# Attention and a residual MLP on one core: a stage's last scalings, nine places for W2's chunks, lam's rows, and the second pass's relus

## The chip, the core and the metric

The kernel runs on one core of a Trainium2 chip. The core has five engines with a queue each: TensorE (PE in the profile, its weight loads PEld), VectorE (DVE), ScalarE (ACT), GpSimd (POOL) and SyncE (SP). POOL and SP issue nearly all DMAs. The metric is the device time of one execution in microseconds, the median of several runs. All durations below are microseconds unless they say ns.

## What is computed

For each of 8 batches, grouped-query attention (16 query heads, 4 key/value heads, 384 positions, head size 64), then an MLP block with residuals on the 384 x 1024 result:

```python
scores = q @ k.T / sqrt(64); attn = softmax(scores); x = attn @ v     # per batch and head
a1 = alpha1 * x + beta1
tok = einsum('ts,bsd->btd', w_tok, a1)
u = x + lam * tok
a2 = alpha2 * u + beta2
ch = maximum(a2 @ w_ch1, 0) @ w_ch2        # 1024 -> 4096 -> 1024
out = u + lam * ch
```

`lam`, `alpha1`, `beta1`, `alpha2` are vectors of 1024. Inputs and the output are float32; the kernel multiplies in bfloat16 and accumulates in float32.

## The kernel before

Five stages run one after the other: `main(0)` and `main(1)` compute the wide MLP of batches 0 and 1, then `pair(0)`, `pair(1)`, `pair(2)` compute that of batches (2,3), (4,5), (6,7). Each stage is a generator that yields after every few matmuls, 0 in its first half (the product with W1) and 1 in its second (the product with W2). A plan written out by hand (`put`, `put_all`) says at which yield the attention work of a later batch is recorded. The instruction order of every engine is the order of recording; nothing is moved by a scheduler.

**The first two stages.** `main(b)` takes W1 in 16 chunks of two 128-column tiles. For each tile, 8 matmuls of 128 x 384 (L531) fill one of two PSUM banks, and a relu with bias writes `hT`: on ScalarE (L540) when the tile's number is even and no exps are near (the counter `exps` is set to 2 by each exp of the attention and counted down by each tile), else on VectorE (L542). TensorE can start a tile only when the relu of the tile before last has freed its bank. In `main(0)` the table `turns` also places small jobs: `to_all` spreads half a row of lam, beta1 or alpha2 over all partitions (a VectorE stream shuffle, L927, of a row that SP loaded at L923), `load_row_set` loads the next such row, `k_transpose` and `q_transpose` turn keys and queries of batch 1 on TensorE. The places count yields: the first four tiles have one yield each (0 to 3), every later tile has two.

**The pair stages.** A pair's two batches are multiplied together, with seven products of half-size blocks instead of eight. The first half runs over eight groups `g`; a group has 14 tiles in the order of `SEQ1`, each of 4 matmuls of 128 x 384 (L724), with products numbered 1 to 7. `LEFT1` names the sum of the left side that a product reads: product 3, the tenth tile, reads `opb(6)`, which VectorE makes at L741, recorded at the fourth tile of group 0. The right sides of group `g+1` are made from two W1 chunks by `sum_w1` (L621, L626) at the tiles 3, 6, 9 and 12 of group `g`. VectorE and ScalarE add up the products (L729 to L737) and make the hidden blocks (L708, L709, L750 to L754). Product 7's and product 4's bank `Y` of the next group is free when L737 is done.

The second half multiplies the hidden blocks with W2 in the order 1, 2, 6, 5, 3, 7, 4 (`PLACE2`), 28 chunks of 512 KB, three row blocks `ms` each (L786). W2's blocks and their sums were written to DRAM tiles `w2s` earlier and are fetched again in each pair stage (L637, on SP). VectorE adds each result (L818 to L825); four of the products give a finished block of the output each. Such a block is scaled by lam in place (L688, 128 x 512 float32) and added to the output in DRAM by an accumulating DMA (`store`, L516, on POOL). Both are put into the list `later` and made one at a time at later points of the second half (`flush(1)`), and all that are left at the stage's end (`flush()`, L831).

**The places.** `w1` has 6 ring places of 512 KB, shared by W1's chunks (loaded on POOL at L185) and W2's. Two more, in `pad`, take every chunk whose number leaves 6 or 7 when divided by 8. `pad`'s 6 parts of 1024 columns also hold the sums of `sum_w1`. `queue` lists all loads in order and `pump` issues its head whenever a place of the right kind is free; while the head has none, the rest waits. Two W1 chunks of the next stage (`heads`) stand before the last two W2 chunks; the next two follow at the head of the next stage's list. Place by place they get their room as the product before is finished.

**What the attention puts in between.** In the pair stages' second half, scores (L279), exps (L288), the product with v (L315), the token product (L340) and their VectorE steps (L320 to L351) are placed between groups of four matmuls, and SP issues DMA transposes and writes of `u` beside the fetches.

Of the kernel before, what the change touches and what calls it, by code (L numbers as in the profile page):

```python
# [12 lines left out]
def kernel(  # L13
# [45 lines left out]
    RING = 6  # L59
# [33 lines left out]
    pad = const.tile([P, 2 * NST * DM], bf, tag="pad", name="pad")  # L93
# [17 lines left out]
    SLOTS = 7 * NH // 4  # L111
# [117 lines left out]
    def side(b):  # L229
# [201 lines left out]
        if not first:  # L431


            turns = {}
            if b == 1:
                turns = {4: [(to_all, 3, 0, 0), (to_all, 3, 1, 1), (load_row_set, 1, 1, 0), (load_row_set, 2, 0, 1)],
                         8: [(k_transpose, 0)], 12: [(to_all, 1, 0, 2), (to_all, 1, 1, 0), (load_row_set, 2, 1, 0)],
                         16: [(scale_beta,)], 20: [(to_all, 2, 0, 1), (to_all, 2, 1, 0)],
                         24: [(q_transpose, 0, 2, "av")], 28: [(k_transpose, 2)]}
                for i in range(3):  # L440
                    turns[32 + 4 * i] = [(q_transpose, 2 + 2 * i, 2, "av")]
            if (b - NPL) // 2 > 0:
                at = {}

                def put(k, *m):
                    at.setdefault(k, []).append(m)

                for j in range(6):
                    put((0, 6, 12, 21, 26, 31)[j], scores3, j, j in (2, 5))
                for p in range(NP):  # L450
                    put((4, 10, 14, 18, 24, 29, 33, 35)[p], av, p)
                    put((8, 15, 17, 22, 27, 32, 36, 38 if b % 2 else 39)[p], tok_flip, p)
                    if by_pe(p):
                        put((36, 39, 41)[p - NP + 3], turn, p)
                return turns, at
            return turns, {
                0: [(scores3, 0)], 4: [(av, 0)], 6: [(scores3, 1)], 8: [(tok_flip, 0)], 11: [(av, 1)],
                13: [(scores3, 2, True)], 15: [(av, 2)], 16: [(tok_flip, 1)], 18: [(tok_flip, 2)], 19: [(av, 3)],
                21: [(scores3, 3)], 23: [(tok_flip, 3)], 25: [(av, 4)], 27: [(scores3, 4)], 29: [(tok_flip, 4)],
                31: [(av, 5)], 33: [(scores3, 5, True)], 35: [(av, 6), (tok_flip, 5)], 37: [(av, 7)],  # L460
                38: [(tok_flip, 6)], 41: [(tok_flip, 7)],
                **{39 + 4 * i - i // 2 * 2: [(turn, p)] for i, p in enumerate((5, 6, 7)) if by_pe(p)}}
# [57 lines left out]
    def main(b):  # L520
# [4 lines left out]
        for i, c in enumerate(seq):  # L525
            for j in range(CW):
                nt = c * CW + j
                begun = b == 0 and nt in early
                ps = early[nt] if begun else bank([P, 512], "mm", "h")
                for dt in range(0 if begun else NDT):  # L530
                    nc.tensor.matmul(out=ps[:, :n], lhsT=w1[:, w1_slots[c], dt, j * P:(j + 1) * P],  # L531
                                     rhs=a2T[:, dt, :n], start=(dt == 0), stop=(dt == NDT - 1))
                    if dt == 3:
                        yield 0
                c1 = bias1[:, nt:nt + 1]
                if b == 0:
                    evac("DVE" if nt % 2 else "ACT")(out=c1, in_=ps[:, S:n])
                exps[0] -= 1
                if nt % 2 == 0 and exps[0] < 0:
                    nc.scalar.activation(out=hT[:, nt, :], in_=ps[:, :S], func=RELU, bias=c1)  # L540
                else:
                    nc.vector.tensor_scalar(out=hT[:, nt, :], in0=ps[:, :S], scalar1=c1,  # L542
                                            scalar2=0.0, op0=ADD, op1=mybir.AluOpType.max)
                yield 0
            if i + RING < NCH:
                w1_free.append(w1_slots.pop(c))
                load_w1(seq[i + RING])

            if b == 0 and i == NCH - RING:
                for dw, r, h in [(0, 1, 1)] + [(0, r, h) for r in (2, 3) for h in range(2)] + [  # L550
                        (1, r, h) for r in range(4) for h in range(2)]:
                    load_w2(dw, r, h)
                load_next(2)
# [74 lines left out]
    NB = (B - NPL) // 2  # L628
    w2_slots, w2_at = {}, {}

    def padded(n):
        return n % 8 > 5

    def fetch(i, n):
        w2_slots[i, n] = slot = (pad_free if padded(n) else w1_free).pop(0)
        w2_at[i, n] = ring[:, slot] if slot < RING else pad[:, (slot - RING + 1) * 2048:(slot - RING + 2) * 2048]
        nc.sync.dma_start(out=w2_at[i, n], in_=w2s[n])  # L637

    def free(slot):
# [3 lines left out]
    def pump():  # L643
        while queue:
            f, *a = queue[0]
            if not (pad_free if f == fetch and padded(a[1]) else w1_free):
                return
            queue.pop(0)
            f(*a)

    pad_free = []
    queue = []
    for i in range(NB):
        heads = [(load_w1, c) for c in order1[:2]] if i + 1 < NB else []
        queue += [(load_w1, c) for c in order1[2 if i else RING:]] + [(fetch, i, n) for n in range(SLOTS - 2)] + heads
        queue += [(fetch, i, n) for n in (SLOTS - 2, SLOTS - 1)]

    IDENT = mybir.ActivationFunctionType.Identity
    SEQ1 = ((1, 0), (1, 1), (7, 0), (6, 0), (6, 1), (7, 1), (5, 0), (5, 1), (2, 0), (3, 0), (3, 1), (2, 1), (4, 0), (4, 1))
    LEFT1 = {1: 3, 2: 4, 3: 6, 4: 1, 5: 2, 6: 5, 7: 0}  # L660
    LEFT2 = {1: 0, 2: 4, 3: 4, 4: 1, 5: 3, 6: 0, 7: 2}

    pair_banks = ExitStack()

    def share_banks(*names):
        pair_banks.close()
# [4 lines left out]
    def pair(i):  # L671
# [19 lines left out]
        def flush(n=9):  # L691
            while later and n:
                f, *a = later.pop(0)
                f(*a)
                n -= 1

        later = []
        last = i == NB - 1

        def sums_hid(o, r):  # L700
# [10 lines left out]
        for g in range(NH // 2):  # L711
            X, Y, snap = {}, {}, {}
            for k, (o, e) in enumerate(SEQ1):
# [16 lines left out]
                if o == 5:  # L730
                    tt(out=hid[:, t, 1], in0=Y[e][:, :S], in1=snap[5, e], op=ADD)
                elif o == 2:
                    tt(out=hid[:, t, 0], in0=ps, in1=snap[1, e], op=ADD)
                elif o == 3:
                    nc.scalar.activation(out=hid[:, t, 4], in_=ps, func=RELU, bias=hi)
                elif o == 4:
                    tt(out=hid[:, t, 2], in0=ps, in1=snap[6, e], op=ADD)  # L737
                if (o, e) in ((2, 1), (3, 1)):
                    free(w1_slots.pop(g if o == 2 else g + NCH // 2))
                if k == 3 and g == 0:  # L740
# [26 lines left out]
        for k, o in enumerate(PLACE2):  # L767
            whole = not last and o != 4
            for h in range(1 if whole else 2):
                for ms in range(NST):  # L770
# [13 lines left out]
                    for (c0, c1, x), t in ((c, t) for c in X[ms] for t in range(8 * h, upto)):  # L784
# [12 lines left out]
                        if t % 4 == 3 and t < upto - 1 and c1 == 512:  # L797
                            q = 4 * ms + t // 4
                            if whole and o in (2, 6) and q in (2, 5, 8, 10):
                                sums_hid(o, (2, 5, 8, 10).index(q))  # L800
                            if t % 8 == 3:
                                flush(1)
                            yield 1
                    if k == ms == h == 0:
                        pad_free[:] = [RING, RING + 1]
                        pump()
                    if (whole or h == 1) and not (last and o == 4):
                        if o in (1, 6, 5):
# [19 lines left out]
                    if last and o in (2, 6) and (h, ms) in ((0, 1), (0, 2), (1, 0), (1, 1)):  # L828
                        sums_hid(o, [(0, 1), (0, 2), (1, 0), (1, 1)].index((h, ms)))
                    yield 1  # L830
        flush()  # L831

    order = {mybir.EngineType.PE, mybir.EngineType.DVE, mybir.EngineType.Activation,
             mybir.EngineType.Pool, mybir.EngineType.SP}
# [221 lines left out]
```

## Time and profile before

| what | value |
|---|---|
| runs | 742.67, 743.75, 743.16; median 743.16 |
| profiled execution | 742.75, its span 741.0 |
| busy, share of the span | PE 98%, DVE 70%, PEld 56%, ACT 43%, POOL 22% |
| `main(0)`, `main(1)` | to about 132, to about 243 |
| `pair(0)`, `pair(1)`, `pair(2)` | from about 243, 416 and 591 |
| DMA | 151.32 MB, mean 204 GB/s |
| busy from 205 to 230, then 230 to 338 | DVE 18.13 of 25; 86.26 of 108 |

A matmul's end is modelled, so TensorE's busy share does not say that it runs at its peak. Lines of the timeline give the start, the time to the end of the last of a run, the engine, the line of the kernel, the operation, what it writes and reads, the count, and in brackets the idle time before it with what ended it. Lines of the waits give the total, the number of times and the longest. POOL's and SP's queues hold DMAs that wait for what they read and for the place they write; a DMA that waits holds up those behind it in its queue.

### The profile page before, as it was taken

How to read it: one execution, taken by the hardware profiler on the slowest of the kernel's cores; microseconds unless marked ns; L12 is line 12 of the kernel's file. 1: busy time of each engine (PE TensorE's matmuls, PEld its weight loads, DVE VectorE, ACT ScalarE, POOL GpSimd, SP SyncE). 2: the span in 40 equal slices, each digit the busy share in tenths (PEclk: the TensorE clock that was granted, in tenths of full speed). 3: DMA queues.
4: the chain of work that ended last, by engine and by line, in shares of the span. 5: the costliest groups of instructions: out<-in, count | busy, mean ns of one | idle time of the engine just before them, and what ended most of it. 6: DMA issues, size and time to landing. Idle time of an engine off the chain costs nothing.

```text
span 741.0 us, 14454 instructions
## 1 busy us (share of the span) xinstructions
PE 727.3 (98%) x5710; PEld 418.0 (56%) x5769; DVE 521.7 (70%) x1004; ACT 319.5 (43%) x458; POOL 163.4 (22%) x211
## 2 busy tenths in 40 slices
PE   8999999999999999999999999999999999999997
PEld 5856555666555566655555556655555556654444
DVE  7863366577687889749777977747958987762354
ACT  7622431434332566653334366664343256660000
POOL 9434220420000232211011533210002231000011
PEclk9999999999999999999999999999999999999999
DMA  9999999999998999999979999998999999936975
GB/s 187 194 201 200 207 218 175 186 198 181 221 271 244 182 221 213 252 248 211 281 186 251 152 196 180 196 205 199 266 238 201 195 179 119 158 120 231 289 219 97
DMA packets 218018, 151.32 MB, mean 204 GB/s; under 512 B 88661, under 2 KB 197061, under 8 KB 217949
## 3 DMA queue, kind: packets, MB, share of 16 engines
q0 software_dynamic: 120304, 64.60, 66.3%
q1 hardware_dynamic: 97100, 85.39, 41.7%
q8 instruction: 45, 0.74, 0.4%
q10 hardware_dynamic: 544, 0.39, 0.2%
q14 instruction: 25, 0.20, 0.1%
HBM read 154.84 MB, written 38.27 MB: 261 GB/s over the span
## 4 chain that ended last, share of the span: by engine, by line
PE 81%; DMA 7%; DVE 5%; issue 4%; POOL 3%; POOLq 0%; DVEq 0%
PE C L786 24%; PE X L724 15%; PE ch L569 10%; PE h L531 10%; PE Y L724 8%; PE sc L279 4%; PE Z L724 4%; PE sc L315 3%; DMA w<-in_moe_w_ch_dram 3%; PE sc L340 3%; DMA q_raw<-in_q_dram 2%; DMA ops<-a 1%; POOL w L185 1%; DVE xr L323 1%; DMA rows<-in_moe_lam_dram 1%
## 5 line engine op out<-in xcount | busy, mean ns | idle before, releaser
L288 ACT ACTIVATE es<-sc 128x1024 bf16<-128x1024 f32 x126 | 121.4, 1023 | 161.8 <-PE sc L279 150.5
L786 PE MATMUL C<-w,arena 128*128 128x512 bf16 (+2 forms) x779 | 179.6, 373 | 1.8 <-issue 0.3
L786 PEld LDWEIGHTS <-arena 128*128 128x128 bf16 x1040 | 94.7, 98 | 100.5 <-issue 5.1
L729 ACT ACTIVATE hT<-X,bias 128x384 f32<-128x384 f32 x144 | 83.9, 582 | 62.2 <-PE X L724 55.0
L724 PEld LDWEIGHTS <-w 128*128 128x128 bf16 x768 | 75.0, 98 | 51.8 <-DVE ops L741 1.6
L569 PE MATMUL ch<-arena,hT 128*128 128x512 bf16 x366 | 87.9, 379 | 1.0 <-issue 0.3
L185 POOL DMA_DIRECT2D w<-in_moe_w_ch_dram x68 | 61.4, 910 | 123.2 <-PE X L724 70.9
L516 POOL DMA_DIRECT2D out_dram<-hT x33 | 29.1, 883 | 265.3 <-DVE hT L688 91.9
L531 PE MATMUL h<-ops,w 128*128 128x384 bf16 (+1 forms) x480 | 83.3, 327 | 1.6 <-DVE hT L542 1.5
L724 PEld LDWEIGHTS <-pad 128*128 128x128 bf16 x576 | 56.3, 98 | 37.8 <-issue 0.8
L724 PE MATMUL X<-ops,w 128*128 128x384 bf16 x384 | 70.3, 326 | 0.8 <-DVE ops L741 0.8
L724 PE MATMUL X<-ops,pad 128*128 128x384 bf16 x384 | 70.3, 326 | 0.0
L531 PEld LDWEIGHTS <-w 128*128 128x128 bf16 x480 | 45.4, 98 | 31.2 <-issue 2.4
L569 PEld LDWEIGHTS <-hT 128*128 128x128 bf16 x384 | 34.8, 98 | 36.8 <-issue 2.5
L786 PE MATMUL C<-pad,arena 128*128 128x512 bf16 (+2 forms) x220 | 52.5, 371 | 0.2
L347 DVE TENSOR_TENSOR xr<-sc,xr 128x384 f32<-128x384 f32 x56 | 30.9, 553 | 22.8 <-PE sc L340 22.8
L315 PEld LDWEIGHTS <-es 128*128 128x128 bf16 x1008 | 38.3, 97 | 12.4
L340 PEld LDWEIGHTS <-wtokT 128*128 128x128 bf16 x576 | 37.5, 98 | 11.8 <-DVE a L330 0.8
L279 PE MATMUL sc<-qT,kT 64*128 64x384 bf16 (+2 forms) x576 | 41.8, 271 | 1.8 <-ACT hT L288 0.2
L320 DVE RECIPROCAL rinv<-sc 128x6 f32<-128x6 f32 x56 | 10.8, 192 | 42.5 <-PE sc L315 42.3
L315 PE MATMUL sc<-v,es 128*128 128x65 bf16 x1008 | 39.8, 193 | 0.0
L724 PE MATMUL Y<-ops,w 128*128 128x384 bf16 x192 | 39.4, 326 | 0.3 <-DVE arena L737 0.3
(138 smaller groups left out, 909.1 us busy)
## 6 DMA issues: line engine op xcount, KB each, us to landing
w<-in_moe_w_ch_dram POOLq DMA_DIRECT2D x68, 512.0 KB, 10.4
w<-w2s SPq DMA_DIRECT2D x66, 512.0 KB, 4.9
out_dram<-xr SPq DMA_DIRECT2D x56, 192.0 KB, 5.9
pad<-w2s SPq DMA_DIRECT2D x18, 512.0 KB, 7.6
out_dram<-hT POOLq DMA_DIRECT2D x33, 256.0 KB, 5.8
arena<-in_moe_w_ch_dram POOLq DMA_DIRECT2D x16, 512.0 KB, 19.8
w2s<-arena SPq DMA_DIRECT2D x28, 256.0 KB, 3.6
q_raw<-in_q_dram POOLq DMA_DIRECT2D x28, 192.0 KB, 11.0
```

What stands on the lines that cost most here:

```text
L185: nc.gpsimd.dma_start(out=w1[:, w1_slots[c]], in_=w1src[:, :, c * CW * P:(c + 1) * CW * P])
L279: nc.tensor.matmul(out=sc[:, hh, k % 4:k % 4 + n], lhsT=kT[r, 2 * p // G, BLK[hh][sk], :], rhs=qT[r, p, st:st + n, :], start=True, stop=True)
L288: nc.scalar.activation(out=e, in_=sc, func=EXP, scale=scale_qk)
L315: nc.tensor.matmul(out=av[:, hh, sq, :], lhsT=ess[k // 4][:, m % 2, k % 4, :], rhs=vb[:, sk, hk, :], start=(sk == 0), stop=(sk == NST - 1))
L340: nc.tensor.matmul(out=ps[:, tt, :], lhsT=wtokT[:, st, tt * P:(tt + 1) * P], rhs=a1s[p][:, st, :], start=(st == 0), stop=(st == NST - 1 an ...
L347: nc.vector.tensor_tensor(out=u, in0=ps, in1=u, op=ADD)
L516: nc.gpsimd.dma_start(out=at, in_=o, accum_op=ADD)
L531: nc.tensor.matmul(out=ps[:, :n], lhsT=w1[:, w1_slots[c], dt, j * P:(j + 1) * P], rhs=a2T[:, dt, :n], start=(dt == 0), stop=(dt == NDT - 1))
L569: nc.tensor.matmul(out=ps, lhsT=hT[:, nt, ms * P:(ms + 1) * P], rhs=w2[:, row(nt)[0], row(nt)[1], cs], start=(i == 0), stop=(i == NNT - 1))
L724: nc.tensor.matmul(out=ps, lhsT=tb[g, o][:, dt, e * P:(e + 1) * P], rhs=opb(LEFT1[o])[:, dt], start=(o in (1, 2, 7) and dt == 0), stop=(dt ...
L729: nc.scalar.activation(out=snap[o, e], in_=ps, func=IDENT, bias=hi if o == 5 else lo)
L786: nc.tensor.matmul(out=x, lhsT=hid[:, t, LEFT2[o], ms * P:(ms + 1) * P], rhs=rhs[:, t % 4 * 512 + c0:t % 4 * 512 + c1], start=((not last o ...
```

## The change

Four edits.

1. **Last scalings.** `later` lives beside the stages instead of in one, so what is left of it at a stage's end passes to the next; only the last stage empties it at its end. Product 4's three blocks are no longer scaled within their own stage (unless it is the last): each is scaled and stored after the eighth tile of groups 1, 2 and 3 of the next stage.
2. **Nine places.** `pad` gives three places; chunks 6, 7, 8, 15, 16, 17, 24 and 25 go there, in place of 6, 7, 14, 15, 22, 23. The third place covers the parts of `pad` with the sums of the even groups' first two products. Four heads of W1 instead of two are queued before the end of a stage: two before the last two W2 chunks, two behind them.
3. **lam's rows.** In `main(0)` the jobs of one yield are spread over two: the two shuffles of lam from yield 4 to 5 and 7, the second halves of beta1 and alpha2 from 12 to 14 and from 20 to 22, with the loads that follow them; the first key transpose goes from 8 to 9, `scale_beta` from 16 to 17.
4. **Relus.** In `main(1)` every tile away from exps has its relu on ScalarE, not the even ones alone. Nine of its 32 relus change engines; nine were on ScalarE already.

In POOL's queue, the order at a border between pair stages changes from "8 stores, W1, W1, ..." to this: the loads of W1's third and fourth chunk stand one store earlier, the fifth and sixth directly behind product 7's last store, and the three moved stores each behind two or more loads of the next stage (W1's chunks for groups 2 and 3, and k, q and v of a later batch) and before the loads for groups 4, 5 and 6.

```diff
             if b == 1:
-                turns = {4: [(to_all, 3, 0, 0), (to_all, 3, 1, 1), (load_row_set, 1, 1, 0), (load_row_set, 2, 0, 1)],
-                         8: [(k_transpose, 0)], 12: [(to_all, 1, 0, 2), (to_all, 1, 1, 0), (load_row_set, 2, 1, 0)],
-                         16: [(scale_beta,)], 20: [(to_all, 2, 0, 1), (to_all, 2, 1, 0)],
+                turns = {5: [(to_all, 3, 0, 0), (load_row_set, 1, 1, 0)], 7: [(to_all, 3, 1, 1), (load_row_set, 2, 0, 1)],
+                         9: [(k_transpose, 0)], 12: [(to_all, 1, 0, 2)], 14: [(to_all, 1, 1, 0), (load_row_set, 2, 1, 0)],
+                         17: [(scale_beta,)], 20: [(to_all, 2, 0, 1)], 22: [(to_all, 2, 1, 0)],
                          24: [(q_transpose, 0, 2, "av")], 28: [(k_transpose, 2)]}
...
-                if nt % 2 == 0 and exps[0] < 0:
+                if (b or nt % 2 == 0) and exps[0] < 0:
                     nc.scalar.activation(out=hT[:, nt, :], in_=ps[:, :S], func=RELU, bias=c1)
...
-    def padded(n):
-        return n % 8 > 5
+    PADDED = (6, 7, 8, 15, 16, 17, 24, 25)
 
     def fetch(i, n):
-        w2_slots[i, n] = slot = (pad_free if padded(n) else w1_free).pop(0)
-        w2_at[i, n] = ring[:, slot] if slot < RING else pad[:, (slot - RING + 1) * 2048:(slot - RING + 2) * 2048]
+        w2_slots[i, n] = slot = (pad_free if n in PADDED else w1_free).pop(0)
+        w2_at[i, n] = ring[:, slot] if slot < RING else pad[:, (slot - RING) * 2048:(slot - RING + 1) * 2048]
...
-            if not (pad_free if f == fetch and padded(a[1]) else w1_free):
+            if not (pad_free if f == fetch and a[1] in PADDED else w1_free):
...
-        heads = [(load_w1, c) for c in order1[:2]] if i + 1 < NB else []
-        queue += [(load_w1, c) for c in order1[2 if i else RING:]] + [(fetch, i, n) for n in range(SLOTS - 2)] + heads
-        queue += [(fetch, i, n) for n in (SLOTS - 2, SLOTS - 1)]
+        heads = [(load_w1, c) for c in order1[:4]] if i + 1 < NB else []
+        queue += [(load_w1, c) for c in order1[4 if i else RING:]] + [(fetch, i, n) for n in range(SLOTS - 2)] + heads[:2]
+        queue += [(fetch, i, n) for n in (SLOTS - 2, SLOTS - 1)] + heads[2:]
...
-    pair_banks = ExitStack()
+    pair_banks, later = ExitStack(), []
...
-        later = []
         last = i == NB - 1
...
+                if k == 7 and 0 < g < 4:
+                    flush(1)
                 if (o, e) in ((2, 1), (3, 1)):
                     free(w1_slots.pop(g if o == 2 else g + NCH // 2))
...
-                            if t % 8 == 3:
+                            if t % 8 == 3 and later and (last or later[0][1] != 4):
                                 flush(1)
...
-                        pad_free[:] = [RING, RING + 1]
+                        pad_free[:] = [RING + 1, RING + 2, RING]
...
-        flush()
+        if last:
+            flush()
```

## The prediction

> **What bounds the kernel now.** I read the page first, then the waits of TensorE, then the timeline around each of those waits. Durations are microseconds.
>
> ```profile
> span 741.0 us, 14454 instructions
> PE 727.3 (98%) x5710; PEld 418.0 (56%) x5769; DVE 521.7 (70%) x1004; ACT 319.5 (43%) x458; POOL 163.4 (22%) x211
> PE   8999999999999999999999999999999999999997
> PEclk9999999999999999999999999999999999999999
> PE 81%; DMA 7%; DVE 5%; issue 4%; POOL 3%; POOLq 0%; DVEq 0%
> ```
>
> TensorE has work in nearly every slice, at the full granted clock, and the chain is 81% TensorE. None of the edits removes a matmul, so the change can only win back what TensorE waits. The waits name that stock:
>
> ```profile
> PE warm L840 <- DVE wtokT L843: 1.5, 1, 1.5
> PE h L531 <- DVE hT L542: 1.5, 2, 0.8
> PE X L724 <- DVE ops L741: 0.8, 2, 0.5
> PE Y L724 <- DVE arena L737: 0.3, 1, 0.3
> ```
>
> The first is the start of the program and is not touched. The other three lie where the diff works. A shown gap understates its price: matmul ends are modelled, a 384-column matmul is drawn with 0.326 (its group's mean), but eight of them follow one another in 1.30, 0.163 each (the chain has "PE X L724 x8" at 1.30). A wait shown as G therefore moves the next start by G + 0.16. So the stock is 0.80+0.16 at 41.22; 0.65+0.16 at 181.26; 0.14+0.16 at 153.59; 0.26+0.16 at 422.66; 0.06+0.16 at 433.95; 0.30+0.16 at 437.01; 0.54+0.16 at 597.46: 0.96, 0.81, 0.30, 0.42, 0.22, 0.46, 0.70, together 3.87, or 0.5% of the time. That is the ceiling.
>
> **Part 1, lam's rows spread later (first stage).** The timeline of the first stage:
>
> ```profile
> 39.12 0.73 DVE L927 STREAM_SHUFFLE vecs<-rows 128x512 f32<-128x512 f32 x1
> ...
> 39.75 0.72 DVE L927 STREAM_SHUFFLE vecs<-rows 128x512 f32<-128x512 f32 x1
> ...
> 40.55 0.62 DVE L542 TENSOR_SCALAR hT<-h,bias 128x384 bf16<-128x384 f32 x1
> ...
> 41.22 9.97 PE L531 MATMUL h<-ops,w 128*128 128x385 bf16 x60 [0.80 <-DVE hT L542]
> ```
>
> VectorE stands at the first shuffle until 39.09, when the DMA of lam's row lands, does both, and only then the relu that frees TensorE's bank. The instruction order shows that in the changed kernel this relu, with its bias copy, stands between the two shuffles; on VectorE that is the only swap in this stage. The first shuffle still waits for its DMA (not moved). The second shuffle's place costs 0.66 (39.75 less 39.09): relu to 39.89 from 40.55, TensorE resumes at 40.56. The key transpose moves from the middle of a tile to its end; its 6 matmuls still run before 40.26, so TensorE keeps a wait of 0.30. Gain 0.66. The SP loads of the next rows move with their shuffles: the one behind the second shuffle is issued about 0.7 later (40.51 now), and lands, after the 4 to 5 that such loads take, well before its use at 48.70. Bounds: 0 (if lam's DMA lands so late that the relu is last anyway) and 0.96.
>
> **Part 2, last scalings in the next stage (two stage borders).**
>
> ```profile
> 418.31 0.69 DVE L688 TENSOR_TENSOR hT<-hT,vecs 128x512 f32<-128x512 f32 x1
> ...
> 419.63 0.69 DVE L688 TENSOR_TENSOR hT<-hT,vecs 128x512 f32<-128x512 f32 x1
> ...
> 421.65 0.95 DVE L741 TENSOR_TENSOR ops<-ops 128x1536 bf16<-128x1536 bf16 x1
> ...
> 422.66 1.74 PEld L724 LDWEIGHTS <-w 128*128 128x128 bf16 x12 [0.65 <-DVE ops L741]
> ```
>
> From 410 to 422.6 VectorE never stops; L741 is at the end of that backlog and TensorE wants its result. Three L688 stand in front (416.18, 418.31, 419.63); each takes 0.61 from its start to the next one's. Without them L741 starts at 421.65 - 1.83 = 419.8 and ends at 420.8, while TensorE asks at 422.2: the wait is gone with 1.4 to spare. At the second border the same three stand before an L741 at 596.45; 1.83 earlier is 594.6, done at 595.6, asked for at 596.8, again gone (W1's chunk, for which L626 waits 0.40 there, comes earlier by part 3). Gain 0.42 + 0.70 = 1.12; bounds 0 and 1.12.
>
> Where the work goes: one L688 after the eighth tile of groups 1, 2 and 3 of the next stage, 0.61 each. Group 3 of the stage shows the room: VectorE idles 0.54 before L731 and 0.30 before L733, and the first L737 is done about 0.75 before TensorE needs that bank (454.4 against 455.21); 1.6 in all, so 0.61 fits, and 1.0 is left. I cost it at nothing; uncovered it would be six times 0.61, 3.7. Each scaling takes its accumulating store along, 256 KB on POOL's queue; in the new order these stand behind the loads for groups 2 and 3, ahead of W1's chunks for groups 4, 5 and 6.
>
> **Part 3, nine places and four W1 heads.** Two of the last W2 chunks now sit in pad, so the third and fourth W1 chunk of the next stage get ring places when the sixth product ends (about 404) instead of during the seventh:
>
> ```profile
> 409.77 0.92 POOL L185 DMA_DIRECT2D w<-in_moe_w_ch_dram  x1 [1.01 <-PE C L786]
> ...
> 419.89 1.21 POOL L185 DMA_DIRECT2D w<-in_moe_w_ch_dram  x1
> ...
> 432.01 0.69 DVE L626 TENSOR_TENSOR pad<-w 128x1024 bf16<-128x1024 bf16 x1 [2.68 <-DMA w<-in_moe_w_ch_dram]
> ...
> 437.01 0.81 PE L724 MATMUL Y<-ops,w 128*128 128x384 bf16 x4 [0.30 <-DVE arena L737]
> ```
>
> A W1 load issued at 419.89, landing 12.04 later, holds VectorE for 2.68, and the chain of waits runs from it through L626, L731 and L737 to TensorE's waits at 433.95 and 437.01. In the new order that load has no scaling's store ahead of it in POOL's queue; it waits only for its slot, which TensorE frees at 416.2, so it is issued near 417.2, 2.7 sooner, with two stores of 256 KB fewer in front (landings now are 1.3 apart where a store lies between). Landing: 417.2 + 12.04 = 429.2 at today's latency, against 429.33 where VectorE now begins to wait. Gain 0.22 + 0.46 = 0.68, bounds 0 and 0.68. At the second border the same lateness is 1.02 and costs TensorE nothing now. W2's other chunks are fetched one place earlier; TensorE shows no wait on them today, so this is worth nothing.
>
> **Part 4, relus of the second pass.** Nine of them change from VectorE (0.62) to ScalarE (0.58); ScalarE is busy 26.17 of the 67 between 138 and 205, so 5.2 more fits. But the two waits there belong to relus that stay: the first two after each batch of exps remain on VectorE.
>
> ```profile
> 180.59 0.61 DVE L542 TENSOR_SCALAR hT<-h,bias 128x384 bf16<-128x384 f32 x1
> ...
> 181.26 1.46 PE L531 MATMUL h<-ops,w 128*128 128x384 bf16 x8 [0.65 <-DVE hT L542]
> ```
>
> This relu is the first after a late exp, and stands behind a run of six VectorE operations that starts only when TensorE's L315 ends (177.64). Nothing in front of it is removed. I take 0; bounds -0.6 (one exp 0.58 late with an attention product waiting) and +1.11 (both waits gone).
>
> **Sum.** 0.66 + 1.12 + 0.68 = 2.46. The profiled execution took 742.75 (741.0 span, 1.75 around it) and would take 740.3; it lies 0.41 under the median of the three runs, so against 743.16 I forecast 740.7.
>
> **The rivals.**
>
> Only part of it. The waits move instead of going: group 2's W1 chunk is still late, the scaling of group 1 adds 0.61 to the same chain, and part 3 gives nothing: 743.16 - 0.66 - 1.12 = 741.4. For it: loads take up to 14.24 from issue to landing in this stretch (the one of 425.32). Against: fewer bytes ahead.
>
> More than that. The lighter VectorE queue of the second pass also loses the wait at 181.26: 740.7 - 0.81 = 739.9. For it: nine of the 23 relus that VectorE has there leave; against: the six operations before it stay.
>
> It does nothing that counts. DMA is the pace of the stage's first half (its engines are busy nine tenths in nearly every slice), and what TensorE gains at 422.66 it waits for at later W1 chunks, which come as now: 743.16 less only part 1's 0.66 and up to that back, 742.5 to 743.2. For it: W1's chunks for groups 3 and 5 land 0.44 and 0.76 after VectorE wants them (439.58, 458.13). Against: those delays reach TensorE nowhere today.
>
> Slower: the moved stores delay W1. A store costs the queue 1.3. If each adds that to the chunks behind it and the earlier start gives nothing back, group 4's chunk (now landing 448.18, wanted 448.27) is 1.2 late, group 5's 0.76 + 2.6 = 3.4, group 6's 2.3 (now 1.6 early). Less a slack of 1.0 with a scaling and 1.6 without, TensorE loses 0.2 + 1.8 + 0.7 = 2.7 per border, 5.4 in all: 740.7 + 5.4 = 746.1. It decides from 1.6 of lateness on. Against it: today all three stores are already ahead of these same chunks in the same queue. The Trainium skill (DMA: Bandwidth & Descriptors, section Queues, rings and completion order) says that a DMA engine takes one queue's descriptors in ring order but alternates between queues packet by packet; by the first half this rival falls, by the second, SP's traffic could still stretch the loads. The trace agrees with the first half: POOL's transfers issued from 417.16 to 421.37 land in their order, 422.31 to 434.21.
>
> **How the numbers follow.** Forecast 0.52, partial 0.14, more 0.08, nothing 0.16, slower 0.10. Runs of this kernel spread by 0.15%, so 0.2%, 1.5, is about what can be told from no change; faster then means under 741.7. Forecast, partial and more lie there, 0.74, of which I move 0.03 to same for the partial case near the edge: 0.71, 0.19, 0.10. Range: 739.5 (all of the stock but 0.2) to 743.7 (nothing gained, upper run of before); it leaves out the slower case and little else.
>
> **What would show it.** Right: no wait at the ninth tile of stages four and five on L741; VectorE's wait for W1 in group 1 of the fourth stage under 1; TensorE's wait near 41 at 0.1 to 0.3; the wait near 181 still there; L688 after L731 in groups 1 to 3 with no TensorE wait on L737 behind it. Wrong: TensorE waits on L626 or L737 in groups 3 to 5, with VectorE waiting for W1; or waits on exps in the second pass.

## The result and the profile after

| kernel | median | lowest to highest | profiled execution | its span |
|---|---|---|---|---|
| before, in the same call | 743.24 | 742.67 to 743.75 | 742.75 | 741.0 |
| changed | 740.38 | 739.96 to 740.96 | 740.56 | 738.8 |

Six runs of each. The ratio is 0.9963, with a 95% interval of 0.995 to 0.9975: 2.86 us gained, where 2.46 were forecast. The two profiled executions differ by less, 2.19.

From the page of the changed kernel: the span, the busy times, TensorE's clock, and the chain that ended last, by engine.

```profile
span 738.8 us, 14511 instructions
PE 731.5 (99%) x5769; PEld 418.8 (57%) x5769; DVE 516.9 (70%) x995; ACT 324.1 (44%) x467; POOL 163.5 (22%) x211
PEclk9999999999999999999999999999999999999999
PE 95%; DVE 2%; DMA 1%; ACT 0%; issue 0%; DVEq 0%
```

The clock is the same. TensorE's share of the chain went from 81% to 95%, and DMA's from 7% to 1%: the chain no longer leaves TensorE at the stage borders to follow a load of W1. That TensorE is busy 4.2 longer than before says nothing: the trace of before holds 5,710 of the 5,769 matmuls, the new one all. The nine relus are seen to have changed engines (DVE 1004 to 995, ACT 458 to 467).

TensorE's waits in the changed kernel (engine and line waiting, what it waited for; total, times, longest):

```profile
PE warm L841 <- DVE wtokT L844: 1.5, 1, 1.5
PE h L531 <- DVE hT L542: 0.7, 1, 0.7
PE sc L279 <- DVE xr L323: 0.3, 1, 0.3
```

Both waits of the borders, on L741 and on the last additions of a group, are no longer in the list, and of the two on relus one is left. The code behind the edits has moved by up to two lines: what was L724, L729, L731, L737, L688, L927 is now L722, L727, L729, L735, L687, L928; L741 and L626 keep their numbers. The timeline of the changed kernel at the three places that the prediction shows:

```profile
39.24 0.72 DVE L928 STREAM_SHUFFLE vecs<-rows 128x512 f32<-128x512 f32 x1
...
40.04 0.62 DVE L542 TENSOR_SCALAR hT<-h,bias 128x384 bf16<-128x384 f32 x1
40.59 0.72 DVE L928 STREAM_SHUFFLE vecs<-rows 128x512 f32<-128x512 f32 x1
40.96 5.23 PE L531 MATMUL h<-ops,w 128*128 128x385 bf16 x31
...
180.65 0.61 DVE L542 TENSOR_SCALAR hT<-h,bias 128x384 bf16<-128x384 f32 x1
...
181.32 1.46 PE L531 MATMUL h<-ops,w 128*128 128x384 bf16 x8 [0.66 <-DVE hT L542]
...
418.95 0.68 DVE L626 TENSOR_TENSOR pad<-w 128x1024 bf16<-128x1024 bf16 x1
...
419.55 0.95 DVE L741 TENSOR_TENSOR ops<-ops 128x1536 bf16<-128x1536 bf16 x1
...
422.10 1.46 PE L722 MATMUL X<-ops,w 128*128 128x384 bf16 x8
...
428.67 0.68 DVE L626 TENSOR_TENSOR pad<-w 128x1024 bf16<-128x1024 bf16 x1
...
431.84 0.68 DVE L687 TENSOR_TENSOR hT<-hT,vecs 128x512 f32<-128x512 f32 x1
432.44 0.55 DVE L731 TENSOR_TENSOR arena<-Z,hT 128x384 bf16<-128x384 f32 x1
...
432.82 0.90 POOL L516 DMA_DIRECT2D out_dram<-hT  x1 [5.42 <-DVE hT L687]
...
435.75 0.81 PE L722 MATMUL Y<-ops,w 128*128 128x384 bf16 x4
```

A line of TensorE without brackets has not waited, or too shortly to be listed; in the trace itself no matmul of the changed kernel between 405 and 680 has 0.02 or more of idle time before it. Near 41 the relu stands between the shuffles and TensorE goes on; near 181 its wait is as before. At the border L741 runs at 419.55 instead of 421.65, and TensorE's use at 422.10 finds it done. L626 of group 1 starts at 428.67 without a wait, where it had waited 2.68. The scaling L687 of group 1 stands behind the first addition L729, as the edit says, and the `Y` tile at 435.75 does not wait for it.

**A ledger.** Both traces hold 5,769 weight loads in (nearly) the same order, so the n-th load of one can be set against the n-th of the other: how much later it starts. The table gives how this offset from the profiled execution of before changes over each stretch (negative: time won), worked out from the starts in the traces, for all kernels of this study except two that are shown later. The columns of one row hold to about 0.02. Stretch A is the start, to about 34; B the wait near 41; C from there to 417; D the first border, 417 to 440; E to 592; F the second border, 592 to 600; G the rest.

| kernel | A | B | C | D | E | F | G | sum |
|---|---|---|---|---|---|---|---|---|
| changed | +0.70 | -0.97 | +0.32 | -1.30 | -0.04 | -0.89 | 0.00 | -2.18 |
| changed, in a later call | +0.70 | -0.97 | +0.15 | -1.30 | -0.02 | -0.89 | 0.00 | -2.33 |
| part 2, L741 recorded earlier, `e9` | +0.24 | -0.73 | +0.13 | -1.30 | +0.81 | -0.89 | 0.00 | -1.74 |
| parts 2 and 3, `e5` | +0.69 | -0.97 | +0.03 | -1.30 | +0.11 | -0.89 | +0.01 | -2.32 |
| part 1, `e1` | +0.48 | -0.98 | +0.11 | -0.11 | -0.03 | -0.10 | -0.02 | -0.65 |
| part 2, `e2` | +0.49 | -0.87 | +0.69 | +0.28 | +0.49 | +0.01 | 0.00 | +1.09 |
| part 3, `e3` | +0.56 | -0.97 | +0.23 | +0.17 | -0.03 | -0.48 | +0.68 | +0.16 |
| part 4, `e4` | +0.26 | -0.27 | 0.00 | +0.07 | -0.03 | +0.15 | +0.02 | +0.20 |
| part 4 and a line, `e10` | +0.11 | +0.32 | -0.32 | -0.73 | +0.21 | +0.12 | +0.02 | -0.27 |
| changed and a line, `e6` | +0.28 | -0.98 | -0.81 | -1.31 | +0.18 | -0.89 | +0.02 | -3.51 |
| the same again, `e12` | +0.36 | -0.98 | -0.72 | -1.31 | +0.18 | -0.89 | +0.02 | -3.34 |

Three columns carry the result. D and F are the same to 0.01 in every row with parts 2 and 3 together: 2.19 won at the two borders, forecast 1.10 + 0.70. All columns are set against one execution of before; the rows `e1`, `e4` and `e10`, whose borders are those of before, show how much that matters: their D is -0.11, +0.07 and -0.73, their F -0.10, +0.15 and +0.12. Against the mean of these three and before, D and F together give 2.0 instead of 2.19. B is -0.97 or -0.98 wherever part 1 is in, all of the wait at 41; but it is as large in two of the six other rows, and -0.87 in a third. And A, in which no part of the change works, is worse than in the profiled execution of before for every kernel, with part 1 or without: that execution happened to start early, which is why the two profiled executions differ by less than the medians.

### The profile page after: what moved, and what is told of

Read it like the earlier page. It is cut to its first block, busy times and chain, and to the rows that moved or that the text cites. A ratio compares the mean times of both kernels' runs of the same rounds, so it can differ in the third digit from the quotient of the medians.

```text
span 738.8 us, 14511 instructions
## 1 busy us (share of the span) xinstructions
PE 731.5 (99%) x5769; PEld 418.8 (57%) x5769; DVE 516.9 (70%) x995; ACT 324.1 (44%) x467; POOL 163.5 (22%) x211
## 4 chain that ended last, share of the span: by engine, by line
PE 95%; DVE 2%; DMA 1%; ACT 0%; issue 0%; DVEq 0%
PE C L786 30%; PE X L722 17%; PE h L531 10%; PE ch L569 10%; PE Y L722 8%; PE sc L279 5%; PE Z L722 4%; PE sc L315 4%; PE sc L340 3%; DMA ops<-a 1%; PE h L223 1%; PE tok L340 1%; PE av L315 0%; PE warm L841 0%; PE tp L265 0%; ACT hT L288 0%
## 5 line engine op out<-in xcount | busy, mean ns | idle before, releaser
L786 PE MATMUL C<-w,arena 128*128 128x512 bf16 (+2 forms) x744 | 168.0, 372 | 0.0
L727 ACT ACTIVATE hT<-X,bias 128x384 f32<-128x384 f32 x144 | 83.7, 581 | 61.6 <-PE X L722 54.9
L722 PEld LDWEIGHTS <-w 128*128 128x128 bf16 x768 | 75.1, 98 | 50.0
L569 PE MATMUL ch<-arena,hT 128*128 128x512 bf16 x384 | 90.8, 379 | 0.0
L722 PEld LDWEIGHTS <-pad 128*128 128x128 bf16 x576 | 56.4, 98 | 37.2
L722 PE MATMUL X<-ops,w 128*128 128x384 bf16 x384 | 70.2, 326 | 0.0
L722 PE MATMUL X<-ops,pad 128*128 128x384 bf16 x384 | 70.2, 326 | 0.0
L786 PE MATMUL C<-pad,arena 128*128 128x512 bf16 (+2 forms) x296 | 69.9, 373 | 0.0
L722 PE MATMUL Z<-ops,w 128*128 128x384 bf16 x192 | 39.0, 326 | 0.0
```

Of the source, the lines that this page charges most:

```text
L569: nc.tensor.matmul(out=ps, lhsT=hT[:, nt, ms * P:(ms + 1) * P], rhs=w2[:, row(nt)[0], row(nt)[1], cs], start=(i == 0), stop=(i == NNT - 1))
L722: nc.tensor.matmul(out=ps, lhsT=tb[g, o][:, dt, e * P:(e + 1) * P], rhs=opb(LEFT1[o])[:, dt], start=(o in (1, 2, 7) and dt == 0), stop=(dt ...
L727: nc.scalar.activation(out=snap[o, e], in_=ps, func=IDENT, bias=hi if o == 5 else lo)
L786: nc.tensor.matmul(out=x, lhsT=hid[:, t, LEFT2[o], ms * P:(ms + 1) * P], rhs=rhs[:, t % 4 * 512 + c0:t % 4 * 512 + c1], start=((not last o ...
```

## The experiments

Durations are medians, and ratios are to the kernel before, run on the same chip in the same call, with a 95% interval; the ratio is not the quotient of the two medians and differs from it by up to 0.0007. The kernel before had medians of 742.70 (35 runs), 743.12 (16) and 742.44 (21) in the three calls.

### One part at a time

Four kernels hold one part of the diff each, and the kernel before for the rest.

**Part 1 alone: lam's rows.** Only the hunk of `turns`.

```diff
-                turns = {4: [(to_all, 3, 0, 0), (to_all, 3, 1, 1), (load_row_set, 1, 1, 0), (load_row_set, 2, 0, 1)],
+                turns = {5: [(to_all, 3, 0, 0), (load_row_set, 1, 1, 0)], 7: [(to_all, 3, 1, 1), (load_row_set, 2, 0, 1)],
...
```

> The kernel before with the lam rows spread later, and nothing else. Prediction's theory: TensorE's wait at about 41 us falls from 0.80 to 0.1 to 0.3, everything behind it runs 0.66 earlier, time 742.6 against 743.24. Rival (the start of the program decides: in the profile after, TensorE reached this place 0.73 later and so waited less by itself): the wait shrinks by as much as the start is late and the time stays within 0.2 of before.

Measured: 742.52, ratio 0.9992 [0.9983, 1.0001]. In its profile the wait at 41 is gone. But the kernels that keep the old order there tell how little a single profile says of this wait. In seven executions with the old order, that of before among them, it is there three times: 0.80, 0.54 (`e4`) and 1.12 (`e10`), and four times nothing is shown. A + B is -0.16 in their mean (-0.49 to +0.43), and -0.44 (-0.21 to -0.70) in the mean of the seven executions with the new order, in which the wait is never there. So the edit removes a wait that comes and goes, and in the mean of seven executions each wins 0.3, not 0.66. The wait is there where lam's row comes late and TensorE early. In the three executions with it VectorE idles 0.62 to 1.20 for the row, the first shuffle starts at 39.12 to 39.55, and A is 0 to 0.26. In the four without it VectorE idles 0.13 at most, the shuffle starts at 38.62 to 38.83, and A is 0.24 to 0.69. The timing's interval excludes neither 0 nor 0.66.

**Part 2 alone: scalings.** `later` outside the stage, product 4's scalings after the eighth tile, `flush()` in the last stage only; the ring and the heads as before.

```diff
...
+                if k == 7 and 0 < g < 4:
+                    flush(1)
...
-                            if t % 8 == 3:
+                            if t % 8 == 3 and later and (last or later[0][1] != 4):
...
-        flush()
+        if last:
+            flush()
```

> The kernel before with product 4's scalings and stores made in the next stage, and nothing else (eight places, two heads). Prediction's theory: both waits on opb(6) and the small wait at the third tile of each stage go, 1.12 + 0.4 = 1.5, time 741.7; W1's chunk for group 2 stays late and TensorE still waits 0.68 near 434 and 437. Rival: with the stores gone from POOL's queue the loads of W1 go out sooner by that alone, the late chunk goes too, 2.2 in all, time 741.0.

Measured: 742.83, ratio 0.9995 [0.9986, 1.0005]. The scalings have left the front of the opposite-side sum (here L742), and TensorE waits for it longer than before: 2.1 in two waits. The timeline of part 2 alone at the first border:

```profile
422.32 0.69 DVE L626 TENSOR_TENSOR pad<-w 128x1024 bf16<-128x1024 bf16 x1 [3.03 <-DMA w<-in_moe_w_ch_dram]
...
422.93 0.95 DVE L742 TENSOR_TENSOR ops<-ops 128x1536 bf16<-128x1536 bf16 x1
...
423.94 1.47 PE L723 MATMUL X<-ops,w 128*128 128x384 bf16 x8 [1.41 <-DVE ops L742]
...
430.52 0.69 DVE L626 TENSOR_TENSOR pad<-w 128x1024 bf16<-128x1024 bf16 x1
```

VectorE, now with less to do, stands 3.03 at L626, until W1's fourth chunk lands (issued 411.46, landed 422.30); L742 is behind it in the queue. The same place in the kernel before:

```profile
420.24 0.68 DVE L626 TENSOR_TENSOR pad<-w,pad 128x1024 bf16<-128x1024 bf16 x1
...
421.04 0.69 DVE L626 TENSOR_TENSOR pad<-w 128x1024 bf16<-128x1024 bf16 x1
```

There the chunk landed at 421.02 and L626 started at 421.04: the landing was a second cause of the same lateness. VectorE had been free for only 0.12 (420.24 and 0.68 give 420.92), and the timeline has no brackets for so short a wait. Take the scalings away and the other cause holds. The last line of part 2's timeline is a surprise in the other direction: group 2's chunk, for which group 1's L626 waited 2.68 before, is in time. With the stores of product 4 gone from the front of POOL's queue it was issued at 416.98 instead of 419.89 and landed at 427.58 instead of 431.93. That was to be part 3's work. (The +1.09 of this row of the ledger is mostly not part 2's: 0.74 of it is one wait of TensorE at 133 for a DMA of the attention, which this execution, 743.84, has and that of before has not.)

**Part 3 alone: nine places and four heads.**

```diff
-    def padded(n):
-        return n % 8 > 5
+    PADDED = (6, 7, 8, 15, 16, 17, 24, 25)
...
-        heads = [(load_w1, c) for c in order1[:2]] if i + 1 < NB else []
+        heads = [(load_w1, c) for c in order1[:4]] if i + 1 < NB else []
...
-                        pad_free[:] = [RING, RING + 1]
+                        pad_free[:] = [RING + 1, RING + 2, RING]
```

> The kernel before with nine places and four W1 heads, and nothing else (scalings within their stage). Prediction's theory: the waits near 434 and 437 go, 0.68, time 742.6; the waits on opb(6) stay. Rival: the third and fourth chunk are sooner by 6, but the fifth and sixth, for group 2, still stand behind the stores that wait for VectorE, so the waits near 434 and 437 stay and the time is that of before within 0.2.

Measured: 742.31, ratio 0.9992 [0.9982, 1.0002]. The timeline of part 3 alone:

```profile
422.27 1.74 PEld L723 LDWEIGHTS <-w 128*128 128x128 bf16 x12 [0.44 <-DVE ops L740]
...
431.99 0.69 DVE L626 TENSOR_TENSOR pad<-w 128x1024 bf16<-128x1024 bf16 x1 [3.06 <-DMA w<-in_moe_w_ch_dram]
...
433.93 1.46 PE L723 MATMUL Y<-ops,pad 128*128 128x384 bf16 x8 [0.44 <-DVE arena L730]
...
436.99 0.81 PE L723 MATMUL Y<-ops,w 128*128 128x384 bf16 x4 [0.30 <-DVE arena L736]
```

It is the mirror image. The fourth chunk comes early (issued 403.66, landed 415.74), and the wait for the sum (here L740) shrinks, from 0.65 to 0.44 on the weight load, with the scalings still in front of it. But group 2's chunk stays late: it is issued at 419.68, behind accumulating stores that wait for VectorE's scalings (POOL stands 8.27 before the one at 416.99, and the next, at 419.11, is directly ahead of the load), lands at 431.91, and the chain through L626, L730 and L736 takes back from TensorE what the earlier sum gave. At the second border the same chain appears, where before had none (column G, +0.68).

**Part 4 alone: relus.**

```diff
-                if nt % 2 == 0 and exps[0] < 0:
+                if (b or nt % 2 == 0) and exps[0] < 0:
```

> The kernel before with nine more relus of the second pass on ScalarE, and nothing else. Prediction's theory: TensorE's waits at about 153.6 and 181.3 stay (0.14 and 0.65 as shown), time as before within 0.2. Rival: the lighter VectorE queue ends the wait at 181.3, time 742.4. Other rival: a relu on ScalarE holds up exps, TensorE waits on exps, time 743.8.

Measured: 742.89, ratio 0.9999 [0.9989, 1.0009]. TensorE's waits of part 4 alone:

```profile
PE X L724 <- DVE ops L741: 1.7, 2, 1.0
PE h L531 <- DVE hT L542: 1.2, 2, 0.6
```

One of the two waits on a relu is the one at 41, the other that at 181, with 0.65 shown, as before. Nine relus moved and nothing that TensorE waits for with them: column C is 0.00. The wait on L741, which this part does not touch, is 1.7 in this execution and 0.8 in that of before. Column D is only +0.07 all the same: at 422.66 this execution loses 0.76 more than before, and wins 0.68 back where before waits at 433.95 and 437.01.

### Both border parts together

The changed kernel without parts 1 and 4.

> The kernel before with the scalings in the next stage and the nine places with four heads, without the other two parts. Theory after the first four runs: the two need each other. L741 stands behind two things that end together, VectorE's backlog and the landing of W1's fourth chunk; and group 2's chunk is late because the stores hold POOL. Only both edits remove both, so TensorE's waits on L741, L731 and L737 all go: 2.2 less than before, about 740.5 to 741. Rival (the parts add up, each as measured alone, +0.1 and -0.4): 742.4.

Measured: 740.45, ratio 0.9967 [0.9955, 0.9979]; the changed kernel, in another call, has 0.9971 [0.996, 0.9983]. Two parts that alone cannot be told from nothing, each within 0.1%, give the whole result together. Parts 1 and 4 add nothing that the timing can tell.

### Is it the place of the sum in VectorE's queue?

Part 2's failure was put down to L742 standing behind an L626 that waits for a DMA. If so, recording the sum two tiles earlier, ahead of that L626, must do nearly what part 3 did, without a place or a head more:

```diff
-                if k == 3 and g == 0:
+                if k == 1 and g == 0:
                     tt(out=opb(6), in0=opb(4), in1=opb(5), op=SUB)
```

> The kernel of the second run (scalings in the next stage alone) with opb(6) made two tiles sooner in group 0, so ahead of the L626 that waits for W1's fourth chunk. Theory: in the second run the waits on L742 were those of the DMA, passed on by the order of VectorE's queue; with the sum ahead of it they go (1.41 and 0.7 shown), and the rest of the gain at the borders comes back: about 741.0, near 740.5. Rival (VectorE's backlog itself is the price, or the late chunk holds TensorE at the next place as well): 742.5 or more.

Measured: 741.01, ratio 0.9982 [0.9972, 0.9991], where part 2 alone had 0.9995. The timeline of this kernel:

```profile
417.95 0.95 DVE L742 TENSOR_TENSOR ops<-ops 128x1536 bf16<-128x1536 bf16 x1
...
420.32 0.69 DVE L626 TENSOR_TENSOR pad<-w 128x1024 bf16<-128x1024 bf16 x1 [0.83 <-DMA w<-in_moe_w_ch_dram]
...
421.70 1.46 PE L723 MATMUL X<-ops,w 128*128 128x384 bf16 x8
```

The chunk is still late (issued 410.80, landed 420.30), VectorE still waits for it, and TensorE doesn't: columns D and F are -1.30 and -0.89, the same as with part 3. So the chunk's lateness cost TensorE only through the instruction behind it. What is left is column E, +0.81: later chunks are late here, L626 waits 1.60 and 2.05 for those of groups 4 and 5, and a `Y` tile behind the latter shows 0.30 for L736. That is what the earlier loads of part 3 are worth beyond the sum.

### How much room do the moved scalings have?

The prediction put 1.6 of room into a group of the stage's first half, 1.0 beside the scaling. Two kernels add to the changed one a further scaling, or three, of the same block, whose product nothing reads, ahead of each moved scaling:

```diff
                 if k == 7 and 0 < g < 4:
+                    for _ in range(1 if later else 0):
+                        tt(out=obuf[:, :512], in0=later[0][5], in1=lam_t[:, :512], op=MUL)
                     flush(1)
```

> The changed kernel with one more VectorE multiplication of 128x512 float32 before each of the six scalings in the next stages (its product is not used). Theory: VectorE has room for 1.6 in those groups, 1.22 fits, the time is that of the changed kernel within 0.3 (740.4 to 740.7). Rival (the deferred scalings already lie on TensorE's path): 6 x 0.61 = 3.7 more, 744.1.

Measured: 742.24, ratio 0.9993 [0.9982, 1.0005]. In its profile each of the six groups loses 0.14 to 0.21, 1.1 in all. The profiled execution, 741.34, is one of the faster ones; the median lies 1.8 above that of the two border parts in the same call (740.45), and the runs reach from 740.90 to 743.87. Where the rest of the 1.8 goes, no trace shows.

> The changed kernel with three more such multiplications before each of the six scalings (products not used), 2.44 per group with the scaling. Theory: 0.8 over the room of 1.6, so TensorE waits on L737's bank in six groups, 6 x 0.8 = 5 more than the changed kernel, 745.5. Rival (the room is larger, the second L737 decides or VectorE catches up within the group): under 742.

Measured: 749.89, ratio 1.0096 [1.0082, 1.0111]. Both expectations missed: the room is smaller. The timeline of the kernel with three more, in group 1:

```profile
431.40 2.13 DVE L738 TENSOR_TENSOR obuf<-hT,vecs 128x512 f32<-128x512 f32 x3
...
433.56 0.69 DVE L687 TENSOR_TENSOR hT<-hT,vecs 128x512 f32<-128x512 f32 x1
434.17 0.55 DVE L731 TENSOR_TENSOR arena<-Z,hT 128x384 bf16<-128x384 f32 x1
...
436.31 1.01 DVE L735 TENSOR_TENSOR arena<-Y,hT 128x384 bf16<-128x384 f32 x2
...
436.90 0.81 PE L722 MATMUL Y<-ops,w 128*128 128x384 bf16 x4 [1.43 <-DVE arena L735]
```

From 431.40 on VectorE never stops, and TensorE waits for L735 in all six groups, 8.9 shown in sum. An added scaling takes 0.72 (433.56 less 431.40, by three); the groups lose 1.60 to 1.66 of the 2.16 added, and about 0.2 of the 0.72. Both give the same room, 0.5 beside the scaling. The 1.0 counted the 0.54 for which VectorE idles ahead of the addition that is L731 before and L729 here. That idle time lies in front of the point at which the scaling is inserted: VectorE waits there for ScalarE, and does so whatever comes behind. Without it the same sum gives 0.30 + 0.75 - 0.61 = 0.44. One scaling fits, as forecast; a second in the same place would not.

### What holds the waits of the second pass?

The waits near 154 and 181 stayed because their relus were still on VectorE: the counter `exps` is set to 2 by each exp, and the two tiles after it keep VectorE. One line exempts the second pass's late exps:

```diff
-                exps[0] = 0 if first else 2
+                exps[0] = 0 if first or later else 2
```

It was made on the changed kernel:

> The changed kernel, with the relus that come right behind a late exp on ScalarE too. Theory: the waits near 153.6 (0.14 shown) and 181.3 (0.65 shown) belong to relus behind a late exp that stand behind six VectorE operations; on ScalarE they run as soon as the late exp is done, both waits go, 0.3 + 0.8 = 1.1 less than the changed kernel, about 739.3. Rival: ScalarE is still at the exp or the next exps are held up, TensorE waits on exps instead, 740.4 or more.

Measured: 739.24, ratio 0.9955 [0.9941, 0.997]. The timeline of this kernel at the place of the wait near 181:

```profile
176.62 1.02 ACT L288 ACTIVATE es<-sc 128x1024 bf16<-128x1024 f32 x1 [0.78 <-PE sc L315]
...
179.26 0.58 ACT L540 ACTIVATE hT<-h,bias 128x384 bf16<-128x384 f32 x1 [0.72 <-PE h L531]
179.28 0.56 DVE L351 TENSOR_TENSOR a<-xr,vecs 128x384 bf16<-128x384 f32 x1
179.61 1.46 PE L531 MATMUL h<-ops,w 128*128 128x384 bf16 x8
```

ScalarE is through with the exp at 177.64, and at 179.26, after idling 0.72, takes the relu that TensorE wants, while VectorE has yet to begin the last of its six operations; TensorE's tile at 179.61 has no wait before it. Column C is better by 0.8 than that of parts 2 and 3, and by 0.9 to 1.1 than those of the changed kernel.

And on the kernel before with part 4:

> The kernel before with more relus of the second pass on ScalarE, those right behind a late exp among them, and nothing else. Theory: the waits near 153.6 and 181.3 go, 1.1 less than before. But what TensorE reaches sooner must not be lost again at the stage borders: the W1 chunks there are set by TensorE itself, so the 1.1 lasts, 742.0. Rival: the borders are paced by DMA and eat it, 743.

Measured: 742.03, ratio 0.9993 [0.9984, 1.0002], undecided. That the number is the expected one is luck: in this call it is 0.4 under before, not 1.1. The profile shows the same two waits gone (the offset falls by 1.10 across them), and then 0.67 lost again (0.61 shown) to a DMA transpose that TensorE had not had to wait for:

```profile
188.51 0.83 PE L279 MATMUL sc<-qT,kT 64*128 64x384 bf16 x12 [0.61 <-DMA qT<-q_raw]
```

In the two executions of the changed kernel with the line this wait did not appear. Whether it takes a part of the gain in other executions was not tried further.

The changed kernel, and the same with the line, were then run again side by side:

> The changed kernel once more, beside the next one. Theory: 0.9963 of before, as measured.

> The changed kernel with the relus behind a late exp on ScalarE, once more, beside the changed kernel. Theory: 1.1 less than the changed kernel of the same call (ratio 0.9985 between the two). Rival: the same within 0.3.

Measured: 740.27 (739.92 to 740.53), ratio 0.9971 [0.996, 0.9983]; and 739.33 (738.97 to 739.60), ratio 0.9959 [0.9946, 0.9971]. No run of the one reaches into the other's. The line is worth 0.94, and the kernel with it beats both.

## Why the prediction was right, and where its steps were not

**What bounds the kernel.** Right: what was won is waits of TensorE. But 3.87 was not the ceiling, because it left out waits too short for the list; one such is named next. The rule that a wait shown as G costs G + 0.16 held: the changed kernel's offset falls by 0.44, 0.22, 0.46 and 0.71 at 422.66, 433.95, 437.01 and 597.46, where the prediction has 0.42, 0.22, 0.46 and 0.70. The Trainium skill (Perfetto Trace Analysis, section Tensor Engine Instruction (MATMUL, LD_WEIGHTS)) says that TensorE's end is estimated from the instruction's size rather than observed; the trace agrees, 0.326 drawn against 0.163 from one start to the next.

**The sum at the borders, 1.12 + 0.68 = 1.80: mis-sized by 0.39.** The ledger has 1.30 + 0.89 = 2.19. The difference is one tile at each border, the third of group 0, at 418.18 and 592.70 in the trace of before: the offset falls there by 0.19 and 0.18. TensorE waited there for VectorE's sums with the scalings among them; 0.02 of it is idle time in the trace, too little to be in the list from which the stock was made, and by the prediction's own rule 0.02 is 0.18 paid. Against the mean of the four executions with the old borders the miss is smaller, 2.0 against 1.80.

**Which part wins what: wrong.** The step that failed is "Without them L741 starts at 421.65 - 1.83 = 419.8", taken as a gain of part 2; that W1's chunk also had to come earlier was said of the second border only. Alone, part 2's L742 starts at 422.93, held by W1's fourth chunk; and part 3's 0.68, the timely chunk for group 2, is won by part 2 (issued 416.98 with the stores gone, 419.68 with the places alone). The waits for group 2's chunk, at 433.95 and 437.01, are gone with part 2 alone; but part 2 alone pays more than that at L742. Part 3 alone makes the wait on the sum smaller, leaves those for group 2's chunk, and adds the same at the second border. For all of them to go it takes both parts, or part 2 with the sum recorded earlier. The sum over the parts was right only because both are in. The landing at 421.02, next to L626's start at 421.04, was to be read in the trace of before. The signs that the prediction named for the borders all came; the tile that it calls the ninth there, product 3's first, is the tenth.

**Part 1, 0.66: too large by half, on the evidence of the executions.** The mechanism is right, and where the edit is in, the wait was gone in all seven profiled executions, where 0.1 to 0.3 was to be left. The size was read from one execution, in which the start was early and the row late; the mean over seven is 0.3, and part 1's own time, 0.9992 [0.9983, 1.0001], excludes neither this nor 0 nor 0.66. That the total of 2.46 came near 2.86 is then luck in part: in the ledger the 0.39 too little at the borders and the 0.36 too much here nearly cancel.

**Part 4, nothing: right, for the reason given.** Both relus stayed on VectorE behind the same operations, and the one line that moves them wins about what the two waits were priced at: 0.30 + 0.81 = 1.11, against 0.94 measured.

**The scalings cost nothing: right, with half the room.** 0.5 is left, not 1.0.

**The rivals.** "Only part of it" did not come: group 2's chunk landed at 425.03, 3.6 before L626 wanted it. "More than that", by the wait at 181 going too, did not come: it shows 0.66 still. "Nothing that counts" named later chunks as the pace; behind the first border L626 waits 0.92, 1.62 and 0.58 for those of groups 4, 5 and 6 (447.93, 457.76, 465.80), and TensorE waits for none of it. "Slower", by the moved stores ahead of W1's chunks, put this lateness at 1.2, 3.4 and 2.3 and had it reach TensorE from 1.6 on. The lateness is there, but smaller: the chunk behind the first moved store was issued at 434.52 and landed at 447.84, against 434.74 and 448.18 before, while TensorE is by then 1.3 further. The limit fits: 1.62 cost nothing here, and 2.05 cost 0.56 in `e9`. Behind a moved scaling, where the prediction has 1.0, a wait of 1.60 cost `e9` 0.26. POOL's transfers issued between 400 and 440 landed in the order of their issue in all fourteen traces, as the prediction's reading of the queue has it.

**What stays open.** The third place and the two further heads were not tried apart. Nor was the start-up, column A, explained: +0.11 to +0.56 in most kernels and +0.69 to +0.77 in four (the kernel with one more scaling has +0.77), among them one without part 1; no run tells whether part 1 has a share in it.

## What to carry to other kernels

Before an edit is priced from the wait that the profile names, look at when everything else that the waiting instruction, and those ahead of it in its queue, need became ready: a load that lands just as the engine arrives shows no idle time and takes the wait over as soon as the named cause is gone. Try edits on one border together as well as alone; here each alone could not be told from nothing, and both were worth 0.3%. Idle time is room for an inserted instruction only behind the point of insertion, and a wait on an early DMA wants more than one execution before it gets a price.

## What the runs showed of the hardware

Loads of W1, 512 KB each on POOL's queue, took 5.6 to 15.3 from issue to landing between 400 and 620, in five traces. The Trainium skill (DMA: Bandwidth & Descriptors, section Anatomy of one DMA) gives a fit for one transfer from POOL, by which an estimate is 3.2 for the 512 KB written, or 4.4 for the float32 bytes read; under this kernel's traffic no load came down to either. The second chunk of group 2 alone took from 8.29 (changed) to 12.23 (part 3 alone), by what stood before it.

The runs of the kernel before spread more than the first three said: 741.53 to 744.77 over 35 runs, 0.4%. The changed kernel's spread from 739.92 to 740.96 over both calls, and the last one's from 738.97 to 739.60 in its second. The kernels in which a late load of W1 can still reach TensorE are the wide ones (part 2 alone 741.81 to 744.00), and so is the one with one more scaling, whose room is used up (740.90 to 743.87). That the borders' waits on loads make the spread is argued from this and from the columns D and F, which are alike to 0.01 where no load is waited for; no run was made to show it.
